# Attention output of head pairs, turned to feature-major by the DMA crossbar instead of TensorE

## The chip, the cores and the metric

The kernel runs on one core of one Trainium2 chip. A core has TensorE (matrix multiplication; the profile splits it into PE, the matmuls, and PEld, the weight loads beside them), VectorE (DVE), ScalarE (ACT), GpSimd (POOL), SyncE (SP, which here only issues DMAs) and 16 DMA engines. Each engine works through its own instruction stream in order and waits for others by semaphores. The metric is the device time in microseconds (us) of one execution; lower is better.

## What is computed

Block-sparse attention over 4 batches of 8 heads (768 tokens, head size 64), followed by a gated feed-forward network with a short convolution along the tokens:

```python
# q, k, v: [4, 8, 768, 64]; mask from neighbouring, first, last and sampled 32-token blocks
scores = where(mask, (q @ k^T) / 8, -1e9)
attn   = softmax(scores)
o      = attn @ v                                   # [4, 8, 768, 64]
x      = o.transpose(0, 2, 1, 3).reshape(4, 768, 512)

h    = maximum(x @ w_in, 0)                         # w_in [512, 1024]
conv = sum over k=0..2 of conv_w[k] * h shifted by k-1 tokens
out  = (h * sigmoid(conv)) @ w_out                  # w_out [1024, 512]
```

Inputs and outputs are float32; the matmuls work on bfloat16.

## The kernel before

The kernel is written in a tile framework: the program lists the operations, and when it is built the framework lays out the order of each engine's stream from dependencies, buffers and its own estimates of durations. So the order in the trace is not always that of the program text.

**Attention, one head per iteration (line 292, 32 iterations).** The loads of q, k and v (lines 57, 58, 64; on GpSimd's DMA queue, with a cast to bfloat16) run three heads ahead. `qk_stage(it+1)` prepares the next head: six TensorE transposes of q and k side by side into the PSUM tile `tq` (line 154) and two VectorE copies to `Qst` and `Kst` (lines 155, 156). `core(i)` works on six key chunks of 128: two matmuls give `st`, the scores of a chunk against all 768 queries (lines 166, 168; the mask is carried in 24 extra rows), ScalarE takes the exponential to `pt` (line 171), and six small matmuls (line 184) add this chunk's part to `o`, a tile [128 tokens, 6, 65] in which column 64 is the sum of the weights. `st` has two buffers, so that the matmuls run one chunk ahead of the exponentials.

**From the attention output to x transposed.** In iteration `it` the output of head `it-1` is finished in three steps. `xstage_a` (line 190): VectorE takes the reciprocal of column 64 (line 193) and multiplies, giving `xtok` [128 tokens, 6, 64] in bfloat16 (line 196). `xstage_b` (line 199): six TensorE transposes by an identity matrix (line 203) into the PSUM tile `tx` [64, 768]. `xstage_c` (line 206): VectorE copies `tx` to the upper or lower 64 rows of `xT[b][fc]` (line 211). Each `xT[b][fc]` is [128 features, 768 tokens] and holds two heads, `fc = h // 2`. `tx` shares its PSUM tag `pmix` (two buffers) with `tq` and with `o2` of the feed-forward network. In the text `xstage_a` stands ahead of `core` and the other two behind it.

**The feed-forward network of batch b runs beside the attention of batch b+1** as fillers handed to `core`. In the first four iterations of its turn (called m1 in this document) `moe1_a` (line 213) multiplies `w_in` with `xT[b][0..3]` to `hp` (lines 217, 219; for each of 8 output chunks, over the 4 feature chunks in order) and ScalarE applies relu to `hT` (line 222); VectorE does the convolution (lines 228 to 231), ScalarE a tanh (line 238), VectorE the gate to `gT` (line 244). The first `moe1_a` of a batch stands one iteration ahead, so it is the first reader of the last `xT` of its batch. In the other four iterations (m2) `moe2` (line 251) multiplies `gT` with `w_out` to `o2` (line 254), VectorE copies it to `o2s` (line 260, two buffers), and SP stores it (line 261). The plan of lines 263 to 287 says which filler goes where; two `moe2` of batch 2 are left for behind the loop (line 323).

**The end.** For batch 3 nothing is left to overlap with. Behind the last head's three steps and the two `moe2` come eight units: matmuls to `lo` and `hi` (lines 338, 340; first readers of `xT[3][3]` at their fourth feature chunk), relu (346, 347), convolution (354, 356, 362, 364), tanh, gate, and the matmuls with `w_out` (369); then six copies (394, 396) and stores (397).

SP's DMA queue carries three small loads at the start, the block indices and the stores.

Of the kernel before, what the change touches and what calls it, by code (L numbers as in the profile page):

```python
# [9 lines left out]
BF16 = mybir.dt.bfloat16  # L10
I32 = mybir.dt.int32
AF = mybir.ActivationFunctionType
ALU = mybir.AluOpType
# [3 lines left out]
def kernel(  # L17
# [11 lines left out]
    nc = tc.nc  # L29

    B, H, S, D = q.shape
    NB = 24
    NCH = S // 128
# [7 lines left out]
    sb = ctx.enter_context(tc.tile_pool(name="sb", bufs=1))  # L41
    ps = ctx.enter_context(tc.tile_pool(name="ps", bufs=1, space=bass.MemoryType.PSUM))
# [7 lines left out]
    xtok_t = {}  # L50
# [19 lines left out]
    ident = sb.tile([128, 128], BF16, tag="ident")  # L70
# [75 lines left out]
    xT = [[sb.tile([128, S], BF16, tag=f"xt{b}_{fc}", name=f"xt{b}_{fc}") for fc in range(NFC)] for b in range(B)]  # L146
# [43 lines left out]
    def xstage_a(i):  # L190
        o = o_t.pop(i)
        rcp = sb.tile([128, NCH], FP32, tag="rcp", bufs=2, name="rcp")
        nc.vector.reciprocal(out=rcp, in_=o[:, :, 64])
        xtok = sb.tile([128, NCH, 64], BF16, tag="xtok", bufs=2, name="xtok")
        rcp_b = rcp.unsqueeze(2).broadcast_to([128, NCH, 64])
        nc.vector.tensor_tensor(out=xtok, in0=o[:, :, 0:64], in1=rcp_b, op=ALU.mult)  # L196
        xtok_t[i] = xtok

    def xstage_b(i):
        xtok = xtok_t[i]  # L200
        tx = ps.tile([64, S], BF16, tag="pmix", bufs=2, name="tx")
        for j in range(NCH):
            nc.tensor.transpose(out=tx[:, 128 * j:128 * j + 128], in_=xtok[:, j, :], identity=ident)  # L203
        xtok_t[i] = tx

    def xstage_c(i):
        b, h = divmod(i, H)
        tx = xtok_t.pop(i)
        fc = h // 2
        r0 = 64 * (h % 2)  # L210
        nc.vector.tensor_copy(out=xT[b][fc][r0:r0 + 64, :], in_=tx[0:64, :])  # L211

    def moe1_a(b, ffc):
        hp = ps.tile([128, S], FP32, tag="st", bufs=2)
# [77 lines left out]
    for it in range(NITER):  # L292
        i = it
        if it + 3 < NHEADS:
            loads(it + 3)
        if it == 3:
            loads_w()
        if it + 1 < NHEADS:
            qk_stage(it + 1)
        if i >= 1:  # L300
            xstage_a(i - 1)

        pe_fill = []
        dve_fill = []
        for bb, ff in m1_of[it + 1]:
            pe_fill.append(lambda bb=bb, ff=ff: moe1_a(bb, ff))
        for bb, tt in m2_of[it]:
            pe_fill.append(lambda bb=bb, tt=tt: moe2(bb, tt))
        for bb, ff in m1_of[it]:
            dve_fill.append(lambda bb=bb, ff=ff: moe1_conv(bb, ff))  # L310

        core(i, pe_fill, dve_fill)
        if i >= 1:
            xstage_b(i - 1)
        for bb, ff in m1_of[it]:
            moe1_gate(bb, ff)
        if i >= 1:
            xstage_c(i - 1)

    xstage_a(NHEADS - 1)  # L320
    xstage_b(NHEADS - 1)
    xstage_c(NHEADS - 1)
    for bb, tt in m2_post:
        moe2(bb, tt, tail=True)
# [103 lines left out]
```

## Time and profile before

| what | value |
|---|---|
| median of 13 runs | 285.08 us |
| lowest and highest run | 282.59 and 286.41 us |
| the profiled execution, whole | 283.37 us |
| its span in the profile | 281.5 us |
| busy: PE, PEld | 241.0 us (86%), 134.6 us (48%) |
| busy: DVE, ACT, POOL | 194.4 us (69%), 202.6 us (72%), 84.5 us (30%) |
| granted TensorE clock, mean | 0.991 |
| DMA packets | 83470, 18.21 MB |

The profile is of one execution. Busy shares are averages over the whole span; matmuls overlap each other in the pipeline, so that a busy PE is not one at its peak. "Releaser" or `<-` names what ended an engine's idle time before an instruction. The chain of waits goes back from the last instruction to what released it at each step. A landing time of a DMA is from its issue to its completion.

By stage the span falls into a start (to about 28 us), attention alone (28 to 65 us), then for each of the batches 0, 1 and 2 an m1 part (from 65, 126 and 187.5 us) and an m2 part (from 98, 160 and 221 us), and the end (from 241.5 us).

### The profile page before, as it was taken

The page shows a single profiled execution, that of the slowest core. Times are in us where ns is not written, and L with a number is a line of the kernel's source. Part 1 is how long each engine was busy: PE and PEld are TensorE (multiplying, and loading weights), DVE is VectorE, ACT ScalarE, POOL GpSimd, SP SyncE. Part 2 cuts the span into 40 slices and gives each one's busy share as a digit, 9 for nine tenths or more (in the row PEclk, how much of TensorE's full clock was granted, in tenths as well). Part 3 has the DMA queues.
Part 4 walks back from the last instruction along what each step waited for, and adds up shares of the span by engine and source line. Part 5 has one row for each costly group of instructions (what it writes and reads, how often), then busy time and mean ns, then how long its engine had stood idle before and what let it go on. Part 6 is the DMA issues. An engine that isn't in the chain of part 4 may idle for free.

```text
span 281.5 us, 5869 instructions
## 1 busy us (share of the span) xinstructions
PE 241.0 (86%) x2370; PEld 134.6 (48%) x2370; DVE 194.4 (69%) x322; ACT 202.6 (72%) x274; POOL 84.5 (30%) x120
## 2 busy tenths in 40 slices
PE   0399898899888999999888999998998999879870
PEld 0145454456544555555555555555565455444320
DVE  0963435437999994457999975449999963259972
ACT  1058888887898986587788976578788966387621
POOL 8993533633423332241333333332111000000000
PEclk9999999999999999999999999999999999999978
DMA  9999997896664494876766585683622011110005
GB/s 52 67 119 163 185 110 48 56 72 45 42 42 30 30 59 91 115 82 41 82 43 44 33 75 82 107 89 55 44 14 16 0 40 75 42 73 1 0 0 224
DMA packets 83470, 18.21 MB, mean 65 GB/s; under 512 B 78836, under 2 KB 79860, under 8 KB 83444
## 3 DMA queue, kind: packets, MB, share of 16 engines
q0 software_dynamic: 76832, 11.54, 57.7%
q1 hardware_dynamic: 6612, 6.31, 6.8%
q8 instruction: 18, 0.29, 0.4%
q14 instruction: 8, 0.07, 0.1%
HBM read 23.08 MB, written 6.29 MB: 104 GB/s over the span
## 4 chain that ended last, share of the span: by engine, by line
PE 60%; ACT 20%; DVE 10%; issue 6%; DMA 2%; SPq 0%; DVEq 0%; ACTq 0%
ACT pt L171 17%; PE o L184 13%; PE st L166 11%; PE o L254 10%; PE hp L217 8%; PE st L168 5%; PE tx L203 4%; PE hp L219 4%; PE tq L154 3%; DVE cv L362 2%; DVE gt L244 2%; DVE cv L364 2%; DMA cw<-in_moe_conv_w_dram 2%; ACT hT L222 1%; ACT tnh L238 1%
## 5 line engine op out<-in xcount | busy, mean ns | idle before, releaser
L171 ACT ACTIVATE pt<-st 128x768 bf16<-128x768 f32 x192 | 149.2, 808 | 42.6 <-PE st L168 37.1
L184 PE MATMUL o<-vp,pt 128*128 128x65 bf16 x1152 | 68.9, 196 | 12.3 <-ACT pt L171 10.7
L166 PE MATMUL st<-qst,kst 88*128 88x512 bf16 x192 | 75.0, 391 | 3.3 <-DVE qst L125 2.3
L184 PEld LDWEIGHTS <-pt 128*128 128x128 bf16 x1152 | 52.0, 98 | 53.9 <-ACT pt L171 41.0
L57 POOL DMA_DIRECT2D qkb<-in_q_dram x32 | 26.7, 833 | 102.8 <-PE tq L154 93.4
L168 PE MATMUL st<-qst,kst 88*128 88x256 bf16 x192 | 53.1, 277 | 0.0
L211 DVE COPY xt<-tx 64x768 bf16<-64x768 bf16 x32 | 17.5, 548 | 35.5 <-PE tx L203 35.4
L254 PE MATMUL o<-woutb,gt 128*128 128x512 bf16 x144 | 35.2, 379 | 0.0
L64 POOL DMA_DIRECT2D vp<-in_v_dram x32 | 26.7, 834 | 26.8 <-PE o L184 25.3
L217 PE MATMUL hp<-xt,winb 128*128 128x512 bf16 x96 | 32.4, 378 | 2.6 <-ACT pt L171 2.5
L244 DVE SCALAR_TENSOR_TENSOR gt<-tnh,hT 128x768 bf16<-128x768 bf16 x32 | 30.3, 949 | 2.1 <-ACT tnh L238 2.1
L238 ACT ACTIVATE tnh<-cv 128x768 bf16<-128x768 bf16 x32 | 26.9, 841 | 5.4 <-DVE cv L364 4.3
L222 ACT ACTIVATE hT<-hp 128x768 bf16<-128x768 f32 x24 | 19.4, 809 | 13.3 <-PE hp L219 12.6
L154 PE MATMUL tq<-ident,qkb 128*128 128x128 bf16 x192 | 21.4, 229 | 7.4 <-POOL ident masks.py:199 7.4
L58 POOL DMA_DIRECT2D qkb<-in_k_dram x32 | 27.0, 843 | 0.0
L219 PE MATMUL hp<-xt,winb 128*128 128x256 bf16 x96 | 26.1, 272 | 0.0
L229 DVE SCALAR_TENSOR_TENSOR cv<-hT,cw,cv 128x767 bf16<-128x767 bf16 x24 | 24.2, 1009 | 0.5
L231 DVE SCALAR_TENSOR_TENSOR cv<-hT,cw,cv 128x767 bf16<-128x767 bf16 x24 | 24.2, 1007 | 0.2
L203 PE MATMUL tx<-ident,xtok 128*64 128x128 bf16 x192 | 22.7, 227 | 0.9 <-DVE xtok L196 0.9
L168 PEld LDWEIGHTS <-kst 88*128 88x128 bf16 x192 | 19.2, 100 | 4.0 <-issue 3.7
L254 PEld LDWEIGHTS <-gt 128*128 128x128 bf16 x144 | 13.9, 97 | 15.0 <-DVE gt L244 0.4
L203 PEld LDWEIGHTS <-xtok 128*64 128x64 bf16 x192 | 13.0, 109 | 16.3 <-issue 11.5
(60 smaller groups left out, 225.0 us busy)
## 6 DMA issues: line engine op xcount, KB each, us to landing
out_dram<-o2s SPq DMA_DIRECT2D x24, 256.0 KB, 2.0
qkb<-in_q_dram POOLq DMA_DIRECT2D x32, 96.0 KB, 3.0
qkb<-in_k_dram POOLq DMA_DIRECT2D x32, 96.0 KB, 3.4
vp<-in_v_dram POOLq DMA_DIRECT2D x32, 96.0 KB, 3.4
winb<-in_moe_w_in_dram POOLq DMA_DIRECT2D x1, 1024.0 KB, 10.5
woutb<-in_moe_w_out_dram POOLq DMA_DIRECT2D x1, 1024.0 KB, 12.4
cw<-in_moe_conv_w_dram SPq DMA_DIRECT2D x3, 4.0 KB, 3.6
sbi<-in_sampled_blocks_dram SPq DMA_DIRECT2D x1, 0.6 KB
```

Source lines behind the costliest of these rows:

```text
L58: nc.gpsimd.dma_start(out=qkb[:, :, 64:128], in_=k[b, h].rearrange("(c p) d -> p c d", p=128))
L154: nc.tensor.transpose(out=tq[:, 128 * c:128 * c + 128], in_=qkb[:, c, :], identity=ident)
L166: nc.tensor.matmul(out=st[:, 0:512], lhsT=kchunk, rhs=Qst[par][0:88, 0:512], start=True, stop=True)
L168: nc.tensor.matmul(out=st[:, 512:768], lhsT=kchunk, rhs=Qst[par][0:88, 512:768], start=True, stop=True)
L171: nc.scalar.activation(out=p, in_=st, func=AF.Exp, bias=0.0, scale=0.125)
L184: nc.tensor.matmul(out=o[:, j, 0:65], lhsT=ptc[:, 128 * j:128 * j + 128], rhs=Vp[par][:, c, 0:65], start=(c == 0 and j == 0), stop=(c == N ...
L203: nc.tensor.transpose(out=tx[:, 128 * j:128 * j + 128], in_=xtok[:, j, :], identity=ident)
L217: nc.tensor.matmul(out=hp[:, 0:512], lhsT=lw, rhs=xT[b][fc][:, 0:512], start=(fc == 0), stop=(fc == NFC - 1), skip_group_check=True)
L219: nc.tensor.matmul(out=hp[:, 512:768], lhsT=lw, rhs=xT[b][fc][:, 512:768], start=(fc == 0), stop=(fc == NFC - 1), skip_group_check=True)
L238: nc.scalar.activation(out=tnh, in_=cv, func=AF.Tanh, bias=0.0, scale=0.5)
L244: nc.vector.scalar_tensor_tensor(out=gT[ffc], in0=tnh, scalar=1.0, in1=hT, op0=ALU.add, op1=ALU.mult)
L254: nc.tensor.matmul(out=o2, lhsT=gT[ffc][:, 128 * t:128 * t + 128], rhs=woutb[:, ffc, :], start=(ffc == 0), stop=(ffc == NFFC - 1), skip_gr ...
```

## The change

Two heads share one `xtok` tile of [128 tokens, 6, 128]: the even head writes columns 0 to 63 of each chunk, the odd head columns 64 to 127. After the odd head one DMA on SP's queue, with the crossbar's transpose, reads the pair's tile as [128, 768] and writes `xT[b][h // 2]` whole, as [128 features, 6, 128 tokens]. The six TensorE transposes of each head, the PSUM tile `tx` and the VectorE copy are gone; the even head's `xstage_b` and both heads' `xstage_c` do nothing. `xtok` keeps two buffers, which are now pairs of heads.

```diff
         rcp = sb.tile([128, NCH], FP32, tag="rcp", bufs=2, name="rcp")
         nc.vector.reciprocal(out=rcp, in_=o[:, :, 64])
-        xtok = sb.tile([128, NCH, 64], BF16, tag="xtok", bufs=2, name="xtok")
+        if i % 2 == 0:
+            xtok_t[i // 2] = sb.tile([128, NCH, 128], BF16, tag="xtok", bufs=2, name="xtok")
+        xtok = xtok_t[i // 2]
+        r0 = 64 * (i % 2)
         rcp_b = rcp.unsqueeze(2).broadcast_to([128, NCH, 64])
-        nc.vector.tensor_tensor(out=xtok, in0=o[:, :, 0:64], in1=rcp_b, op=ALU.mult)
-        xtok_t[i] = xtok
+        nc.vector.tensor_tensor(out=xtok[:, :, r0:r0 + 64], in0=o[:, :, 0:64], in1=rcp_b, op=ALU.mult)
 
     def xstage_b(i):
-        xtok = xtok_t[i]
-        tx = ps.tile([64, S], BF16, tag="pmix", bufs=2, name="tx")
-        for j in range(NCH):
-            nc.tensor.transpose(out=tx[:, 128 * j:128 * j + 128], in_=xtok[:, j, :], identity=ident)
-        xtok_t[i] = tx
+        if i % 2 == 0:
+            return
+        b, h = divmod(i, H)
+        xtok = xtok_t.pop(i // 2)
+        nc.sync.dma_start_transpose(
+            out=xT[b][h // 2][:, :].rearrange("p (c s) -> p c s", c=NCH),
+            in_=xtok[:, :, :].rearrange("p c s -> p (c s)"))
 
     def xstage_c(i):
-        b, h = divmod(i, H)
-        tx = xtok_t.pop(i)
-        fc = h // 2
-        r0 = 64 * (h % 2)
-        nc.vector.tensor_copy(out=xT[b][fc][r0:r0 + 64, :], in_=tx[0:64, :])
+        pass
```

## The prediction, made before the changed kernel was timed

> **What bounds the kernel now.** First the page: its chain of waits by line.
>
> ```profile
> span 281.5 us, 5869 instructions
> ...
> ACT pt L171 17%; PE o L184 13%; PE st L166 11%; PE o L254 10%; PE hp L217 8%; PE st L168 5%; PE tx L203 4%; PE hp L219 4%; PE tq L154 3%; DVE cv L362 2%; DVE gt L244 2%; DVE cv L364 2%; DMA cw<-in_moe_conv_w_dram 2%; ACT hT L222 1%; ACT tnh L238 1%
> ```
>
> No line has a fifth of the chain; TensorE and ScalarE hand over to each other. The line that goes, L203, has 4%. An average over stages says little, so next comes busy time by stage: 28 to 65 us (attention alone), 65 to 98 (attention beside the first FFN half, "m1"), 98 to 126 (attention beside the second, "m2"). Columns: length, busy time (count) of PE, PEld, DVE, ACT, POOL, then clock, DMA share, GB/s.
>
> ```profile
> 28.00:65.00 37.00, 33.63 (x422) 18.19 (x421) 17.03 (x36) 32.90 (x43) 17.42 (x22) 1.00 1.12 90
> 65.00:98.00 33.00, 29.83 (x305) 17.86 (x305) 30.03 (x48) 28.43 (x39) 10.77 (x15) 1.00 0.58 38
> 98.00:126.00 28.00, 26.98 (x282) 15.04 (x283) 17.08 (x32) 19.87 (x27) 9.10 (x12) 1.00 0.77 89
> ```
>
> In the first ScalarE sets the pace, in m1 three engines are near full, in m2 TensorE is. The chain by line for each stage, in that order, then m1 and m2 of the next two batches (126, 160, 187.5, 221 to 241.5 us):
>
> ```profile
> by line: PE o L184 26.0%; PE st L166 20.0%; ACT pt L171 19.9%; PE tx L203 13.0%; PE st L168 10.4%; PE tq L154 8.4%; issue 2.5%; ACTq L171 0.4%
> ...
> by line: ACT pt L171 26.1%; PE hp L217 23.9%; PE hp L219 10.7%; PE o L184 10.3%; issue 7.4%; PE st L166 7.4%; PE tx L203 5.2%; PE tq L154 3.8%; PE st L168 3.8%; ACT hT L222 3.1%; ACTq L171 0.2%; ACT tnh L238 0.2%
> ...
> by line: PE o L254 32.4%; ACT pt L171 20.5%; PE o L184 16.4%; PE st L166 13.2%; PE st L168 6.9%; PE tq L154 4.7%; issue 3.5%; PE tx L203 2.9%; ACTq L171 0.3%
> ...
> by line: ACT pt L171 25.6%; PE hp L217 23.3%; PE o L184 10.5%; PE hp L219 10.4%; issue 9.2%; PE st L166 7.8%; PE st L168 4.0%; ACT hT L222 3.0%; PE tx L203 3.0%; PE tq L154 2.3%; ACT tnh L238 1.5%; PE o L254 1.3%; ACTq L171 0.1%
> ...
> by line: PE o L254 32.2%; ACT pt L171 23.8%; PE o L184 15.6%; PE st L166 12.7%; PE st L168 7.0%; PE tq L154 3.2%; issue 3.2%; PE tx L203 2.9%; ACTq L171 0.3%
> ...
> by line: PE hp L217 23.7%; ACT pt L171 23.5%; PE hp L219 10.6%; PE o L184 10.3%; issue 9.2%; PE st L166 7.3%; PE st L168 3.7%; ACT hT L222 3.1%; PE tx L203 3.1%; PE tq L154 2.3%; PE o L254 1.9%; ACT tnh L238 1.5%; ACTq L171 0.1%
> ...
> by line: PE o L254 34.3%; PE o L184 17.4%; ACT pt L171 16.0%; PE st L166 13.8%; PE st L168 7.2%; PE tx L203 3.9%; PE hlo L338 2.9%; issue 2.3%; PE tq L154 2.2%; ACTq L171 0.3%
> ```
>
> L203 is on the path in every stage, never for much.
>
> **The change part by part.** Removed are the 192 transposes and 32 copies of these groups (busy time and mean ns, then the engine's idle time before them and what ended it):
>
> ```profile
> L211 DVE COPY xt<-tx 64x768 bf16<-64x768 bf16 x32 | 17.5, 548 | 35.5 <-PE tx L203 35.4
> ...
> L203 PEld LDWEIGHTS <-xtok 128*64 128x64 bf16 x192 | 13.0, 109 | 16.3 <-issue 11.5 <-DVE o2s L260 2.5 <-DVE xtok L196 1.3
> ```
>
> The 17.5 us of VectorE I count at nothing before the tail: L211 waited 35.4 us for TensorE, so it ran in idle VectorE time, and it is on no stage's chain. On m1's full VectorE it is a margin and no term: conv and gate would come earlier, and nothing on that chain waits for them. TensorE time counts only where nothing else is late. With the transposes go their waits for a PSUM buffer that they share with o2 (2.5 us behind o2s); tq takes such a buffer too and may inherit them, so I count none of it and keep 2.5 for the low end.
>
> *Attention alone, 28 to 65 us.* One head's boundary:
>
> ```profile
> 42.05 0.24 PE L203 MATMUL tx<-ident,xtok 128*64 128x128 bf16 x1
> 42.23 0.34 PE L154 MATMUL tq<-ident,qkb 128*128 128x128 bf16 x3
> ...
> 42.75 0.38 PE L166 MATMUL st<-qst,kst 88*128 88x512 bf16 x1
> ...
> 43.34 0.81 ACT L171 ACTIVATE pt<-st 128x768 bf16<-128x768 f32 x1 [0.31 <-PE st L168]
> ```
>
> ScalarE idles 0.31 us per head because st starts late, and one transpose stands before it: 42.23-42.05 = 0.18 us. The other five lie under exponentials. The chain's 13.0% of 37 us (4.8) can't be had, as only 7 x 0.31 = 2.2 us of idle ScalarE exist. Seven heads x 0.18: **1.2 us** (0 to 2.2).
>
> *m1 and m2.* Chain share times length: 0.052x33 = 1.7, 0.029x28 = 0.8, 0.030x34 = 1.0, 0.029x27.5 = 0.8, 0.031x33.5 = 1.0, 0.039x20.5 = 0.8; sum 6.2. An m1 example shows that this is real:
>
> ```profile
> 75.57 0.52 PE L203 MATMUL tx<-ident,xtok 128*64 128x128 bf16 x6
> ...
> 76.42 0.38 PE L217 MATMUL hp<-xt,winb 128*128 128x512 bf16 x1
> ...
> 77.92 0.81 ACT L222 ACTIVATE hT<-hp 128x768 bf16<-128x768 f32 x1 [0.85 <-PE hp L219]
> ```
>
> Six transposes hold hp back while ScalarE idles 0.85 us for it. But each hole closed brings up the next path: the row shows hp released 0.85 us late, of which the transposes are at most 0.52, so other waits remain behind. And the order on TensorE is laid out when the program is built: a head's six transposes stand scattered in attention alone (x1 at 42.05) and in a row in m1 (x6 at 75.57). Without them the planner may put tq, hp or st elsewhere, for better or worse. Between none and all of 6.2 I take three quarters, as most pieces stand before such an idle ScalarE: **4.6 us**.
>
> *Added: 16 crossbar DMAs on SP.* No row shows one. Its pieces are 256 bytes (128 bf16), 768 of them; a load of v or q is 768 rows of 64 float32, also 256 bytes each. Landing times, min/median/max, of the v loads, the q loads and the stores:
>
> ```profile
> DMA to landing us min/median/max: 3.0/3.4/9.3
> ...
> DMA to landing us min/median/max: 2.8/3.0/9.4
> ...
> DMA to landing us min/median/max: 2.0/2.0/3.6
> ...
> q0 software_dynamic: 76832, 11.54, 57.7%
> ```
>
> So a landing L lies between 2.0 and 9.4 us; I take 3.4, the row with as many pieces of the same size. [...] Traffic grows by 16 x 768 = 12,288 packets, at q0's rate 9% of the span; the loads it meets are issued three heads ahead, over 15 us by 37 us for seven heads, which is more than the slowest 9.4. If that cover went, st would wait for a late tq.
>
> SP's queue holds only stores. Where does xT have to be there? At the fourth feature chunk of the first hp of each batch:
>
> ```profile
> 60.10 0.56 DVE L196 TENSOR_TENSOR xtok<-o,rcp 128x384 bf16<-128x384 f32 x1
> ...
> 66.16 0.38 PE L217 MATMUL hp<-xt,winb 128*128 128x512 bf16 x1
> ...
> 121.16 0.69 DVE L260 COPY o2s<-o 128x512 f32<-128x512 f32 x1 [0.75 <-PE o L254]
> ...
> 127.02 0.38 PE L217 MATMUL hp<-xt,winb 128*128 128x512 bf16 x1
> ...
> 182.83 0.69 DVE L260 COPY o2s<-o 128x512 f32<-128x512 f32 x1 [1.03 <-PE o L254]
> ...
> 188.68 0.38 PE L217 MATMUL hp<-xt,winb 128*128 128x512 bf16 x1
> ...
> L261 SPq DMA_DIRECT2D out_dram<-o2s x18: 332/332/367, 105.9 to 247.2; - x18
> ```
>
> Batch 0: 66.16-60.66 = 5.5 us of cover. In batches 1 and 2 the DMA stands in program order behind that iteration's store, which waits for its copy and takes 0.33 us to issue: 127.02-122.18 and 188.68-183.85, 4.8 us each. Behind a DMA on SP wait only later stores. Its issue I price as a store's, 0.33 us, with SP held until the landing (9.4) as the other end: then stores would start that much later, and with two o2s buffers the second copy after it, and so TensorE's o2, would wait. 0.33 is the nearest row, of the same queue. The new wait of xtok for the DMA two pairs earlier has four heads, 21 us, of cover. xtok's write is half-row strided with the same 384 elements from PSUM; I take no change (L196 takes 0.56 us per head, so a 10% change would be 1.8 us of VectorE, mostly idle).
>
> *The end.*
>
> ```profile
> 241.20 0.36 PE L184 MATMUL o<-vp,pt 128*128 128x65 bf16 x6
> 241.82 0.56 DVE L196 TENSOR_TENSOR xtok<-o,rcp 128x384 bf16<-128x384 f32 x1
> 242.43 0.52 PE L203 MATMUL tx<-ident,xtok 128*64 128x128 bf16 x6 [0.88 <-DVE xtok L196]
> 242.89 3.63 PE L254 MATMUL o<-woutb,gt 128*128 128x512 bf16 x16
> ...
> 246.84 0.33 PE L338 MATMUL hlo<-xt,winb 128*128 128x384 bf16 x1
> ```
>
> L254 need no longer wait for tx: it can start at 241.56, and hlo 246.84-242.89 = 3.95 us behind it, at 245.5, if xT is there. The DMA lands at 242.38+L = 245.8. hlo then runs 246.84-245.8 = **1.0 us** earlier; break-even is L = 4.5, and beyond it the end is later by L-4.5, for everything behind follows from hlo.
>
> **Sum:** 1.2+4.6+1.0 = 6.8 us. The profiled execution took 283.37 (span 281.5, 1.9 around it) and would take 276.6; it lies 1.7 below the median 285.08, which becomes 278.3.
>
> **Rivals.**
> *Cover:* the transposes fill holes in which TensorE waits for exponentials anyway.
>
> ```profile
> 116.09 2.46 ACT L171 ACTIVATE pt<-st 128x768 bf16<-128x768 f32 x3 [1.43 <-PE st L168]
> ...
> 116.43 0.47 PE L203 MATMUL tx<-ident,xtok 128*64 128x128 bf16 x5
> 116.96 0.36 PE L184 MATMUL o<-vp,pt 128*128 128x65 bf16 x6
> ```
>
> Here the o matmuls wait for the exponential that ends at 116.91 whatever tx does. Against it stands the 0.85 us hole above. If only the end gains: 285.1-1.0 = 284.1.
>
> *Late landing, the slower side:* L eats the covers 5.5, 4.8, 4.8 and 4.5 (together 19.6). TensorE, in order, stalls 4L-19.6 while the transposes removed still give 5.8: it decides from L = 6.35 on. With the slowest load's L = 9.4 the stalls are 18.0, the time 285.1+12.2 = 297.3. For it: 9.4 occurs, and a transpose may be slower than a copy. Against: that is a load queued behind weights, and at the end no load runs. [...]
>
> *Not what it says:* the DMA breaks into single elements, 128 times the pieces. At q0's rate (57.7% of 281.5 us for 76,832) 1.57 million pieces take 3.3 ms. Nothing but the change's words speaks against it.
>
> **How the numbers follow.** Forecast 0.55, 278.3, own range 274 to 283; cover 0.17, 284.1; late landing 0.26; not what it says 0.02. A measurement of this kernel can tell 0.5%, 1.4 us, from no change. Cover splits half and half between faster and same; late landing leaves 0.04 near its break-even. Faster 0.55+0.08 = 0.63, same 0.09+0.04 = 0.13, slower 0.22+0.02 = 0.24. Low end 273: all of 2.2 and 6.2, 1.3 at the end with L = 2.0 (hlo right at 245.5), and the 2.5 of buffer waits, 12.5 in all, give 272.6, rounded up. High end 289: L = 7.3; beyond it lies some 0.1.
>
> **What would show it.** ScalarE's idle per head below 0.31 us in attention; idle before hT below 0.85 in m1; L by the DMA rows; no stall of hp L217 on a DMA at the three batch starts; hlo right behind L254 at the end. I am wrong if L exceeds 6, or if TensorE's busy time falls with ScalarE's idle time unchanged.

## The result: right in total, by two errors that cancel

The changed kernel takes 278.73 us (median of 11 runs, 276.25 to 280.82) against 285.42 us for the kernel before (48 runs): a ratio of 0.9783, 95% interval 0.9749 to 0.9817, clear of no change and on both sides of a gain of 2%. (Medians are of all runs; the ratios leave out slow ones, those more than 1.5% above the fastest of their kernel.) Predicted were 278.3 us and a range of 273 to 289. The steps to that number were worse than the number: the m2 parts gained six times what they were given (11.7 us for 1.8), m1 gained nothing, and a stall that had no term stands at the start.

From the page of the changed kernel; its profiled execution took 278.73 us as well:

```profile
span 277.0 us, 5494 instructions
...
PE 226.2 (82%) x2178; PEld 123.9 (45%) x2178; DVE 177.3 (64%) x290; ACT 202.0 (73%) x274; POOL 84.7 (31%) x120
...
PEclk9999957999999999999999799999999999999997
...
DMA packets 96270, 21.35 MB, mean 77 GB/s; under 512 B 91636, under 2 KB 92660, under 8 KB 96244
...
q1 hardware_dynamic: 19412, 9.45, 14.2%
...
ACT pt L171 19%; PE o L184 12%; PE st L166 9%; PE o L254 9%; PE hp L217 8%; PE st L168 5%; PE hp L219 4%; DMA qkb<-in_k_dram 4%; ACT hT L222 3%; DVE cv L362 2%; DVE gt L244 2%; DVE cv L364 2%; DMA cw<-in_moe_conv_w_dram 2%; ACT tnh L238 2%; PE tq L154 1%
```

L203 has left the chain of waits, but a load has come into it: `qkb<-in_k_dram`, the k of some head, with 4%. And the clock row has two dents, slices 6 and 7 and slice 23.

To see where the time went, the span is cut at the starts of the VectorE reciprocal (line 193) of the same heads in every kernel: those of heads 3, 8, 12, 16, 20, 24, 28 and 31. The columns are the start, attention alone (five heads), m1 and m2 of batches 0, 1 and 2 (the last m2 has three heads), the end, and the span, in us. Each row is one profiled execution; the experiments, told below, stand in it too.

| kernel | start | att. | m1 b0 | m2 b0 | m1 b1 | m2 b1 | m1 b2 | m2 b2 | end | span |
|---|---|---|---|---|---|---|---|---|---|---|
| before | 38.89 | 26.20 | 33.00 | 27.81 | 33.74 | 27.92 | 33.75 | 20.28 | 39.91 | 281.5 |
| after | 47.19 | 25.00 | 33.27 | 22.90 | 34.63 | 23.99 | 33.36 | 17.41 | 39.25 | 277.0 |
| e1_w_later | 42.61 | 25.01 | 33.27 | 22.91 | 33.36 | 24.01 | 33.36 | 17.41 | 38.96 | 270.9 |
| e2_q2 | 38.70 | 26.19 | 36.59 | 24.93 | 34.35 | 24.20 | 33.99 | 17.97 | 38.98 | 275.9 |
| e3_dma_twice | 49.55 | 25.02 | 33.27 | 22.91 | 33.36 | 24.01 | 33.35 | 17.42 | 38.81 | 277.7 |
| e4_pairs_on_pe | 36.30 | 25.43 | 35.42 | 24.75 | 33.13 | 25.45 | 33.13 | 18.27 | 41.42 | 273.3 |
| e5_w_gate | 37.27 | 25.00 | 33.27 | 22.91 | 33.35 | 24.01 | 33.35 | 17.41 | 38.93 | 265.5 |
| e6_buffer | 39.52 | 25.05 | 34.32 | 26.45 | 35.90 | 26.93 | 37.56 | 21.02 | 40.25 | 287.0 |
| e7_tq_twice | 35.86 | 24.99 | 33.78 | 24.57 | 35.26 | 23.82 | 35.04 | 15.95 | 39.13 | 268.4 |
| e8_copy | 37.24 | 25.00 | 33.74 | 22.43 | 33.27 | 25.21 | 33.26 | 18.61 | 38.94 | 267.7 |
| e9_before_gate | 40.96 | 26.21 | 33.04 | 27.80 | 33.74 | 27.92 | 33.74 | 20.29 | 39.90 | 283.6 |
| e10_pairs_gate | 39.80 | 25.42 | 35.45 | 24.75 | 33.13 | 25.45 | 33.13 | 18.27 | 39.80 | 275.2 |
| e11_dummy_first | 38.68 | 25.02 | 33.72 | 22.91 | 33.35 | 24.01 | 33.37 | 17.41 | 39.63 | 268.1 |

After minus before: start +8.3, attention alone -1.2, m1 +0.3, +0.9 and -0.4, m2 -4.9, -3.9 and -2.9, end -0.7; together -4.5, the difference of the spans. The medians differ by 6.7: the profiled execution of before, 283.37 us, was 2 us faster than its median, that of after stood at its own.

**The start.** TensorE's timeline of after, around its longest idle time:

```profile
31.24 0.27 PE L168 MATMUL st<-qst,kst 88*128 88x256 bf16 x1
38.98 0.37 PE L154 MATMUL tq<-ident,qkb 128*128 128x128 bf16 x2 [7.47 <-DMA qkb<-in_k_dram]
...
39.49 0.62 PE L166 MATMUL st<-qst,kst 88*128 88x512 bf16 x1
```

TensorE stands still for 7.47 us before the tq of a later head, and the st of the current head, whose data are there, waits behind it in the stream. Then st takes 0.62 us in place of 0.38. The windows of the same time (length, busy time and count of PE, PEld, DVE, ACT, POOL, clock, DMA share, GB/s) show the clock of 0.51 that follows:

```profile
31.00:39.00 8.00, 0.53 (x9) 0.17 (x6) 1.11 (x2) 1.40 (x2) 3.75 (x5) 0.73 1.80 166
39.00:45.00 6.00, 6.00 (x52) 4.23 (x52) 0.76 (x2) 3.24 (x4) 2.46 (x3) 0.51 1.71 111
```

Why is k late? GpSimd's timeline has its loads in order:

```profile
19.93 0.85 POOL L140 DMA_DIRECT2D winb<-in_moe_w_in_dram  x1
...
24.09 0.89 POOL L141 DMA_DIRECT2D woutb<-in_moe_w_out_dram  x1
...
24.97 0.83 POOL L57 DMA_DIRECT2D qkb<-in_q_dram  x1
28.19 0.82 POOL L64 DMA_DIRECT2D vp<-in_v_dram  x1 [2.39 <-PE o L184]
29.00 0.83 POOL L58 DMA_DIRECT2D qkb<-in_k_dram  x1
```

The two weights, 1 MB each, are issued at 19.93 and 24.09. The k load issued at 29.00 (counted along the queue, head 7's) is behind them and is waited for until 38.98. In the kernel before nobody needed it then. The windows with tile tq alone, up to the end of the start stage, count the tq transposes, six to a head, in before and in after:

```profile
0.00:38.89 38.89, 4.61 (x36) 1.00 1.40 118
```

```profile
0.00:47.19 47.19, 8.31 (x54) 0.89 1.44 116
```

By head 3's output, before has made tq for 36 / 6 = 6 heads, after for 54 / 6 = 9. The load of k kept its time (before issues it at 29.07); its reader moved three heads ahead.

**m2.** The windows of m2 of batch 0, before and after:

```profile
98.09:125.90 27.81, 26.79 (x282) 14.92 (x282) 16.92 (x31) 19.71 (x27) 8.91 (x12) 1.00 0.77 89
```

```profile
105.46:128.36 22.90, 21.83 (x242) 12.31 (x241) 10.63 (x21) 19.02 (x26) 8.21 (x10) 1.00 0.86 111
```

TensorE is busy for 96% of it before and 95% after: m2 lasts as long as TensorE has work in it. What work that is, the groups by line of the same windows say (busy time and mean ns, then idle time before); before:

```profile
L254 PE MATMUL o<-woutb,gt 128*128 128x512 bf16 x42 | 10.1, 379 | 0.0
...
L154 PE MATMUL tq<-ident,qkb 128*128 128x128 bf16 x24 | 2.7, 221 | 0.0
L203 PE MATMUL tx<-ident,xtok 128*64 128x128 bf16 x24 | 2.7, 226 | 0.0
```

and after:

```profile
L254 PE MATMUL o<-woutb,gt 128*128 128x512 bf16 x31 | 9.6, 379 | 0.0
...
L154 PE MATMUL tq<-ident,qkb 128*128 128x128 bf16 x18 | 2.2, 219 | 0.0
```

Not only the 24 transposes went. Eleven o2 matmuls and six tq transposes left the stage too; the same view of after's m1 of batch 0 has the o2 matmuls, of which before has none there:

```profile
L254 PE MATMUL o<-woutb,gt 128*128 128x512 bf16 x12 | 3.9, 378 | 0.0
```

What one of them costs TensorE is read from rows in which they stand close together, six tx in 0.52 us (at 75.57, in the prediction), six tq in 0.51, eight o2 in 1.89:

```profile
76.02 0.51 PE L154 MATMUL tq<-ident,qkb 128*128 128x128 bf16 x6
...
113.59 1.89 PE L254 MATMUL o<-woutb,gt 128*128 128x512 bf16 x8
```

That is 0.087, 0.085 and 0.24 us. Batch 0: 24 x 0.087 + 6 x 0.085 + 11 x 0.24 = 2.1 + 0.5 + 2.6 = 5.2 us, against 4.9 measured. The counts of all stages, taken in the same way (o2 / tq / tx):

| kernel | m1 b0 | m2 b0 | m1 b1 | m2 b1 | m1 b2 | m2 b2 |
|---|---|---|---|---|---|---|
| before | 0/24/24 | 42/24/24 | 8/24/24 | 42/24/24 | 8/24/24 | 32/6/18 |
| after | 12/12/0 | 31/18/0 | 11/30/0 | 38/18/0 | 11/30/0 | 33/0/0 |
| e2_q2 | 2/24/0 | 42/18/0 | 6/30/0 | 42/18/0 | 6/30/0 | 38/0/0 |
| e4_pairs_on_pe | 4/28/12 | 38/18/12 | 11/30/12 | 38/18/12 | 11/30/12 | 28/0/6 |
| e5_w_gate | 11/12/0 | 27/18/0 | 10/30/0 | 34/18/0 | 9/30/0 | 30/0/0 |
| e9_before_gate | 0/24/24 | 38/24/24 | 7/24/24 | 38/24/24 | 7/24/24 | 30/6/18 |
| e6_buffer | 0/24/4 | 38/24/4 | 6/24/4 | 38/24/4 | 6/24/4 | 30/6/3 |
| e7_tq_twice | 11/26/0 | 27/36/0 | 18/60/0 | 25/36/0 | 18/60/0 | 22/0/0 |

Records are missing in the last four rows: the whole run has 144 o2 matmuls, all of them recorded in the first four kernels, but 129 in e5_w_gate and e7_tq_twice and 133 in e9_before_gate and e6_buffer. So those four are compared only with each other; e9_before_gate has the stage times of before to 0.04 us from attention on, but 38 o2 where before has 42. For batches 1 and 2 the same sum gives 3.6 and 1.8 us, against 3.9 and 2.9. Of the 11.7 us, 66 transposes are 5.7 and work that moved out of m2 is 4.9 (18 tq, 14 o2); 1.1 us are left over.

**m1.** The hole that the prediction took for its example, with what stands before it; before:

```profile
75.57 0.52 PE L203 MATMUL tx<-ident,xtok 128*64 128x128 bf16 x6
75.58 0.79 ACT L222 ACTIVATE hT<-hp 128x768 bf16<-128x768 f32 x1
```

and the same place in after:

```profile
82.28 0.81 ACT L222 ACTIVATE hT<-hp 128x768 bf16<-128x768 f32 x1
...
83.15 0.38 PE L217 MATMUL hp<-xt,winb 128*128 128x512 bf16 x1
...
84.64 0.81 ACT L222 ACTIVATE hT<-hp 128x768 bf16<-128x768 f32 x1 [0.85 <-PE hp L219]
```

The hole is 0.85 us in both. hp starts 0.06 us after the preceding hT ends (82.28 + 0.81 = 83.09), and in before 0.05 us after it (75.58 + 0.79 = 76.37, hp at 76.42): hp and st share one PSUM tag with two buffers (lines 164 and 214), and hp waits for ScalarE to free one. The six tx were over at 76.09, and the six tq of the row at 76.02 follow them; but without either, the buffer was not free before 76.37.

**The landing.** The source's own rows for the DMA (issue time in ns, then the landing):

```profile
L206 SPq DMA_TRANSPOSE xt<-xtok x16: 1212/1223/1667, 28.7 to 238.6; - x16
...
  PE hlo L338: 0.7, 1
...
DMA to landing us min/median/max: 2.7/3.5/8.6
```

Only the first hlo waited for it, 0.7 us, once; no hp did.

### The profile page after: what moved, and what is told of

The parts are those of the page before. It is cut to its first block, busy times and chain, and to the rows that moved or that the text cites. A ratio compares the mean times of both kernels' runs of the same rounds, so it can differ in the third digit from the quotient of the medians.

```text
span 277.0 us, 5494 instructions
## 1 busy us (share of the span) xinstructions
PE 226.2 (82%) x2178; PEld 123.9 (45%) x2178; DVE 177.3 (64%) x290; ACT 202.0 (73%) x274; POOL 84.7 (31%) x120
## 2 busy tenths in 40 slices
DMA packets 96270, 21.35 MB, mean 77 GB/s; under 512 B 91636, under 2 KB 92660, under 8 KB 96244
## 4 chain that ended last, share of the span: by engine, by line
PE 48%; ACT 25%; DVE 10%; issue 8%; DMA 6%; SPq 1%; POOL 0%; DVEq 0%; ACTq 0%
ACT pt L171 19%; PE o L184 12%; PE st L166 9%; PE o L254 9%; PE hp L217 8%; PE st L168 5%; PE hp L219 4%; DMA qkb<-in_k_dram 4%; ACT hT L222 3%; DVE cv L362 2%; DVE gt L244 2%; DVE cv L364 2%; DMA cw<-in_moe_conv_w_dram 2%; ACT tnh L238 2%; PE tq L154 1%
## 5 line engine op out<-in xcount | busy, mean ns | idle before, releaser
L254 PE MATMUL o<-woutb,gt 128*128 128x512 bf16 x144 | 41.7, 379 | 0.0
L155 DVE COPY qst<-tq 64x768 bf16<-64x768 bf16 x32 | 17.5, 547 | 33.1 <-PE st L168 24.1
L217 PE MATMUL hp<-xt,winb 128*128 128x512 bf16 x96 | 33.6, 388 | 3.7 <-ACT hT L222 1.6
L154 PE MATMUL tq<-ident,qkb 128*128 128x128 bf16 x192 | 23.9, 237 | 15.2 <-DMA qkb<-in_k_dram 7.7
L154 PEld LDWEIGHTS <-qkb 128*128 128x128 bf16 x192 | 16.4, 106 | 24.4 <-issue 18.1
L219 PE MATMUL hp<-xt,winb 128*128 128x256 bf16 x96 | 26.7, 278 | 0.0
L193 DVE RECIPROCAL rcp<-o 128x6 f32<-128x6 f32 x32 | 6.2, 193 | 26.6 <-PE o L184 26.2
L168 PEld LDWEIGHTS <-kst 88*128 88x128 bf16 x192 | 19.3, 100 | 5.5 <-issue 5.4
L166 PEld LDWEIGHTS <-kst 88*128 88x128 bf16 x192 | 19.1, 100 | 2.5 <-issue 0.6
```

Of the source, the lines that this page charges most:

```text
L154: nc.tensor.transpose(out=tq[:, 128 * c:128 * c + 128], in_=qkb[:, c, :], identity=ident)
L166: nc.tensor.matmul(out=st[:, 0:512], lhsT=kchunk, rhs=Qst[par][0:88, 0:512], start=True, stop=True)
L168: nc.tensor.matmul(out=st[:, 512:768], lhsT=kchunk, rhs=Qst[par][0:88, 512:768], start=True, stop=True)
L217: nc.tensor.matmul(out=hp[:, 0:512], lhsT=lw, rhs=xT[b][fc][:, 0:512], start=(fc == 0), stop=(fc == NFC - 1), skip_group_check=True)
L219: nc.tensor.matmul(out=hp[:, 512:768], lhsT=lw, rhs=xT[b][fc][:, 512:768], start=(fc == 0), stop=(fc == NFC - 1), skip_group_check=True)
L254: nc.tensor.matmul(out=o2, lhsT=gT[ffc][:, 128 * t:128 * t + 128], rhs=woutb[:, ffc, :], start=(ffc == 0), stop=(ffc == NFFC - 1), skip_gr ...
```

## The experiments

The theory after the first readings: **(P)** the gain is the order of TensorE's stream, in which work can move to better places because nothing of the attention output takes one of the two `pmix` buffers any more; **(W)** its price is that tq runs ahead into loads that queue behind the weights. The rivals: TensorE's time itself (T), VectorE's time (V), the landing (L).

**Weights later.** The request for both weights moved from iteration 3 to 6.

```diff
-        if it == 3:
+        if it == 6:
             loads_w()
```

> The changed kernel with the two weight loads listed three heads later. Theory A (the 7.5 us stall of TensorE at 31.5 us is a k load that queues behind the 2 MB of weights, met because tq now runs several heads ahead): the stall shrinks to 0 to 3 us, the clock stays up, and the time is 270.5 to 273.5. Rival B (the stall comes from the crossbar DMA that starts at 28.7 us beside the loads): the stall stays, 277.5 to 280.

Measured: 274.07 us (4 runs), ratio 0.9639 [0.9569, 0.9709]; start 42.61 in place of 47.19. A stall is left:

```profile
32.03 0.48 PE L154 MATMUL tq<-ident,qkb 128*128 128x128 bf16 x3 [3.53 <-DMA qkb<-in_k_dram]
```

In this execution `woutb` was issued at 30.20, but `winb`, which waits for nothing, still at 19.83. So half of the stall goes with one of the two weights. The time lies between the two brackets: W is supported, not yet settled.

**Shorter lead.** Qst and Kst get two buffers in place of four, so that tq cannot run three heads ahead; the loads stay as in the changed kernel.

```diff
+    NQK = 2
-    Qst = [... for p in range(NPAR)]
-    Kst = [... for p in range(NPAR)]
+    Qst = [... for p in range(NQK)]
+    Kst = [... for p in range(NQK)]
...
-        par = i % NPAR
+        par = i % NQK
```

> The changed kernel with two buffers in place of four for the prepared q and k of a head, so that tq can't run more than about two heads ahead; the weight loads stay where they are. Theory A: the stall goes, 270 to 273. Rival B: it stays, 277.5 to 280, as the crossbar DMAs are the same.

Measured: 277.96 us, 0.9794 [0.9719, 0.987]: a miss in total. The start fell to 38.70 as W expects, but the order changed elsewhere: attention alone is back at 26.19, m2 b0 at 24.93, and m1 b0 took 36.59, with st at 0.62 us from 73.4 to 76.5 and again from 82.9 to 86.4. The edit changes more than the lead, and it shows something of m2. No tx transposes stand there and `pmix` is as free as in the changed kernel, but the o2 matmuls have not moved; the group in m2 of batch 0:

```profile
L256 PE MATMUL o<-woutb,gt 128*128 128x512 bf16 x42 | 11.7, 378 | 0.0
```

That is 42 as in before, and m1 of batch 0 has 24 tq again and only 2 o2 (counts above). By the prices above 24 tx and 6 tq are 2.6 of the 2.9 us between 27.81 and 24.93. So the free buffer alone does not move o2; the longer lead of tq, which this edit cuts, seems to be needed too.

**Twice the transposes by DMA.** Behind each real one a second goes into a tile that nothing reads.

```diff
+        xdum = sb.tile([128, S], BF16, tag="xdum", bufs=2, name="xdum")
+        nc.sync.dma_start_transpose(
+            out=xdum[:, :].rearrange("p (c s) -> p c s", c=NCH),
+            in_=xtok[:, :, :].rearrange("p c s -> p (c s)"))
```

> The changed kernel with each crossbar DMA issued twice, the second into a tile that nobody reads; the order on the engines is that of the changed kernel. If the DMAs run beside everything: within 1 us of the changed kernel, 277.7 to 279.7, with 0.3 to 1.2 us more at the end if the second holds up the first's landing. Rival B: the stall at 31.5 us grows by 1 us or more and SP's 1.2 us per issue delays stores, 281 or more.

Measured: 279.29 us, 0.9827 [0.9771, 0.9883], hardly more than the changed kernel. The table shows it stage by stage: the start is 2.4 us longer, no other stage by more than 0.1. TensorE's wait there:

```profile
PE tq L154 <- DMA qkb<-in_k_dram: 9.8, 1, 9.8
```

9.8 us in place of 7.5. The doubled crossbar traffic goes with a late k load that is later by another 2.3 us, as rival B said of the stall, and costs nothing where loads have cover, so that the total stays in the first bracket. How much of the 7.5 us is the first crossbar DMA's, and not the weights', no run separates.

**Packing without the crossbar.** Two heads share `xtok`, but six TensorE transposes [128 by 128] and one VectorE copy [128, 768] turn the pair.

```diff
-        nc.sync.dma_start_transpose(
-            out=xT[b][h // 2][:, :].rearrange("p (c s) -> p c s", c=NCH),
-            in_=xtok[:, :, :].rearrange("p c s -> p (c s)"))
+        tx = ps.tile([128, S], BF16, tag="pmix", bufs=2, name="tx")
+        for j in range(NCH):
+            nc.tensor.transpose(out=tx[:, 128 * j:128 * j + 128], in_=xtok[:, j, :], identity=ident)
...
+        nc.vector.tensor_copy(out=xT[b][h // 2], in_=tx)
```

> Packing alone: the pair's tile is turned by six 128x128 TensorE transposes and one 128x768 VectorE copy, so half of the removed work of both engines stays, and no crossbar DMA. If the gain goes with TensorE and VectorE work, half of it: 281 to 283, if not more from a stall that is absent. If it goes with the PSUM buffers that the transposes share with tq and o2, less than half: 283 to 285.

Measured: 273.81 us, 0.9632 [0.9566, 0.9698]: both expectations missed, and the version is 4.9 us faster than the one with the crossbar. `pmix` is taken by tx 16 times in place of 32; m2 falls to 24.75, 25.45 and 18.27, about two thirds of the way (76.0 before, 68.5 here, 64.3 after, summed over the batches): half of the transposes are still there, but as many tq as in the changed kernel, and 4 o2 per batch, have left m2 (counts above). And tq does not run far enough ahead to meet a late load (start 36.30).

**Weights held back.** The changed kernel with `winb` requested after head 4's xtok and `woutb` after head 8's; a one-element copy into each makes the load wait (`loads_w` is split in two).

```diff
-        if it == 3:
-            loads_w()
+        if it == 5:
+            nc.vector.tensor_copy(out=winb[0:1, 0, 0:1], in_=xtok_t[(i - 1) // 2][0:1, 0, 0:1])
+            loads_w1()
+        if it == 9:
+            nc.vector.tensor_copy(out=woutb[0:1, 0, 0:1], in_=xtok_t[(i - 1) // 2][0:1, 0, 0:1])
+            loads_w2()
```

> The changed kernel with the two weight loads held back: w_in until head 4 has been written to xtok, w_out until head 8 (a one-element VectorE copy into each ahead of its load). Theory A (loads behind the 2 MB of weights make the stall in the start, 8.3 us by the end of head 3): the start is as before (38 to 39.5 us to the reciprocal of head 3) or earlier and the time is 267.5 to 271. Rival B (the crossbar DMA beside the loads makes it): above 274, the start above 42.

Measured: 268.42 us (267.39 to 269.38), 0.9434 [0.9346, 0.9522], the fastest kernel of this study, 10.3 us under the changed one. The stall is gone, and the windows with tile tq alone show that the lead stayed:

```profile
0.00:37.27 37.27, 7.35 (x54) 1.00 1.44 91
```

So W holds: 54 transposes by head 3 as in after, but no late load, and the start is 9.9 us shorter (47.19 - 37.27): 7.5 of idle TensorE, and 2.4 for which the 6 us at a clock of 0.51 are the likely reason. The second dent of the clock row went too (m1 b1 33.35 in place of 34.63).

**The same for the kernel before, as a control.** The same edit, in the kernel before.

> The kernel before with the weights held back as in e5_w_gate, nothing else. Theory G (the gate only takes away the stall and the crowd of loads that the change brought; the kernel before has neither): start within 1.5 us of its 38.9, the other stages as before, 282.5 to 285.5 us. Rival H (the gate is worth the same 10 us to any version, and then the gain of e5_w_gate says nothing of the change): 273 to 277 us.

Measured: 285.17 us, 1.0011 [0.9964, 1.0058]. G holds: the gate gives the kernel before nothing. Its start is 2.1 us longer in the profiled execution, more than expected; the likely reason is that st is at 0.38 us only from 30.55 on, in before from 24.41 (told at the end). The cost that the gate removes came with the change.

**One buffer per head put back.** e5_w_gate with one small transpose per head into a `pmix` tile and a copy of 64 by 16 out of it, which nothing reads.

```diff
+        tx = ps.tile([64, S], BF16, tag="pmix", bufs=2, name="tx")
+        for j in range(1):
+            nc.tensor.transpose(out=tx[:, 128 * j:128 * j + 128], in_=xt2[:, j, 64 * (i % 2):64 * (i % 2) + 64], identity=ident)
...
+        nc.vector.tensor_copy(out=scr[0:64, 0:16], in_=tx[0:64, 0:16])
```

> e5_w_gate, and each head again takes one of the two shared PSUM buffers for a moment: one of the six transposes (0.08 us of TensorE) and a VectorE copy of 64x16; the result is not used. Theory P (the gain beside the second FFN half, some 4 us per batch, comes from the PSUM buffers that tq and o2 no longer share with the transposes, and so from another order on TensorE): 6 to 11 us slower than e5_w_gate, m2 back near 27 us. Rival T (it comes from TensorE's time): at most 1.5 us slower.

Measured: 287.28 us (10 runs), 1.0081 [1.0029, 1.0133]: by the ratios some 18 us above e5_w_gate, with a sixth of the transposes and a copy of 16 columns per head put back. In the profiled execution the granted clock is 0.95 in m1 of batch 1 and 0.91 and 0.92 in batch 2, so only the parts at 1.00 are used: m2 26.45 and 26.93 for batches 0 and 1, against 22.91 and 24.01 without and 27.81 and 27.92 in the kernel before. The tq count up to head 3's output is that of before:

```profile
0.00:39.52 39.52, 5.35 (x36) 1.00 1.08 69
```

The o2 matmuls in m2 of batch 0, in e5_w_gate and then here:

```profile
L256 PE MATMUL o<-woutb,gt 128*128 128x512 bf16 x27 | 8.6, 379 | 0.1
```

```profile
L264 PE MATMUL o<-woutb,gt 128*128 128x512 bf16 x38 | 9.7, 378 | 0.1
```

38 is what e9_before_gate has there, and in the other stages o2 and tq are those of e9_before_gate too, to one o2. So it is the taking of a buffer, not the size of the work done in it, that decides where o2 and tq stand, and P holds for the placing. By the prices above, 11 o2, 6 tq and 4 tx are 11 x 0.24 + 6 x 0.085 + 4 x 0.087 = 3.5 us, all of the difference in m2 of batch 0 (26.45 - 22.91); in batch 1 4 o2, 6 tq and 4 tx are 1.8 of the 2.9 us, and what the rest is stays open. The 18 us as a whole are more than P expected; m1 at 35.90 and 37.56 ran at a clock of 0.95 and 0.91, so not all of it is order.

**TensorE's time put back, without the buffer.** e5_w_gate with the transposes of q and k each done twice into the same tile: 192 more, as many as the change removed.

```diff
-        for c in range(NCH):
+        for c in list(range(NCH)) * 2:
```

> e5_w_gate, with each transpose of q and k done twice into the same place: TensorE's removed work (six transposes per head) is there again, but no further buffer is taken. Rival T: 5 to 9 us slower than e5_w_gate, m2 back near 27 us. Theory P: 1 to 4 us slower.

Measured: 270.59 us, 0.9506 [0.944, 0.9572]: 2.2 us more. T alone is out: with all of TensorE's work back but no buffer taken, by the ratios some 14 of the 16 us between before and e5_w_gate remain. The counts show how: in m1 of batch 1 there are 60 tq transposes (35.26 us in place of 33.35), and 9 more o2 matmuls have left m2 of batch 1 (25 for 34 in e5_w_gate), which in spite of 18 more tq takes 23.82 us for 24.01. That m2 follows TensorE's work holds here too: in batch 0, where o2 stays, 18 more tq are 1.5 us, and 24.57 - 22.91 = 1.7.

**VectorE's time put back.** e5_w_gate with a copy of 64 by 768 per head, from Kst, which nothing reads.

```diff
+        nc.vector.tensor_copy(out=scr[0:64, :], in_=Kst[i % NPAR][0:64, :])
```

> e5_w_gate, with a VectorE copy of 64x768 per head (from SBUF, about 0.5 us, result unused) where the removed one stood. Theories P and T: within 1 us of e5_w_gate. Rival V (the gain is VectorE's 17.5 us): 3 us slower or more, most of it in m1, where VectorE is at 91%.

Measured: 272.76 us (269.84 to 273.26, 4 runs), 0.9557 [0.947, 0.9645]: 4.3 us more by the medians. The copies from SBUF are shorter than those removed, which took 17.5 us:

```profile
L214 DVE COPY scr<-kst 64x768 bf16<-64x768 bf16 x32 | 12.1, 378 | 0.3
```

The profiled execution is the fastest of the four, and there m1 is as without the copy but for 0.5 us in batch 0, while m2 changes by -0.5, +1.2 and +1.2. V's place, m1, is not supported; that the copies cost nothing isn't either. In m2 of batch 1 VectorE is busy for only 14.9 of the 25.2 us, TensorE has the same 34 o2 and 18 tq as in e5_w_gate, and it waits 2.2 us for exponentials in place of 1.0: the price there is a wait, not a full VectorE. What made that wait, and why the other three runs are 3 us longer, stays open.

**Packing without the crossbar, weights held back.** e4_pairs_on_pe with the gate of e5_w_gate, so that the two can be compared without a stall.

> The packing alone (TensorE transposes and a copy per pair, as e4_pairs_on_pe) with the weights held back as in e5_w_gate, so that neither it nor e5_w_gate has the stall at the start. Theory P (most of the gain comes from freeing the PSUM buffers half as often, the crossbar itself gives the end, 1.5 to 2.5 us, and 1 to 2 us per m2): 271.5 to 274 us, m2 24 to 25.5 us per batch. Rival X (the crossbar gives nothing over packing beside the end): 269.5 to 271 us. Rival T (TensorE time is what counts; half of it is back): 275 to 278 us.

Measured: 275.16 us, 0.9658 [0.9583, 0.9733]. By the total this is T's bracket, by the stages P's: m2 24.75, 25.45 and 18.27, exactly as in e4_pairs_on_pe. Against e5_w_gate it loses 0.4 in attention alone, 2.2 in m1 b0 (granted clock 0.95 in that window), 4.1 in the three m2, 0.9 at the end, and 2.5 at the start, where st is slow until 32.1; the two other m1 are 0.2 us shorter each. Its profiled execution is the slowest of the four, 2.2 us above the median, so these add up to more than the medians differ by. So the crossbar on its own is worth about 6.7 us by the medians (275.16 - 268.42), or 5.4 against the same packing without the gate (273.81); 5.4 of the profiled differences are in attention, m2 and the end. It is worth that only where the loads don't stall it. T's reading, that half of TensorE's time is back, is not separated from the placing by this run alone.

**A later landing.** e5_w_gate with a dummy crossbar DMA ahead of each real one.

```diff
+        nc.sync.dma_start_transpose(
+            out=xdum[:, :].rearrange("p (c s) -> p c s", c=NCH),
+            in_=xtok[:, :, :].rearrange("p c s -> p (c s)"))
         nc.sync.dma_start_transpose(
```

> e5_w_gate with a second crossbar DMA of the same pair, into a tile that nothing reads, issued ahead of each real one, so that xT lands later by at least one issue (1.2 us) and at most one landing (4 us). Theory C (the covers at the batch starts, 4.8 to 5.5 us behind a landing of 4.0, still hold or nearly; only the end follows the landing): the end later by 1 to 4 us, at most 1 us at each batch start, 269.5 to 273 us. Rival L (the landing is already on the path at each batch start): three stalls of 1 to 4 us on the DMA of xt there besides, 274 to 284 us.

Measured: 271.76 us, 0.9539 [0.9479, 0.9599]. TensorE's waits for the landing, in the view of waits (us in total, times, longest):

```profile
PE hlo L348 <- DMA xt<-xtok: 1.6, 1, 1.6
...
PE hp L223 <- DMA xt<-xtok: 0.3, 1, 0.3
```

C holds in the main: with the real DMA issued 1.3 us later, two batch starts still see nothing and one sees 0.3 us; the last hlo waits 1.6 us in place of 0.4. The end grows by 0.7, less than the 1 to 4 that C expected, and the start by 1.4. The medians differ by 3.3 us, at the upper part of C's bracket.

## Why the prediction was right, and where it wasn't

*Attention alone, 1.2 us:* the stage is 1.2 us shorter. From 52.81 on ScalarE has 17 exponentials in a row without waiting for TensorE:

```profile
52.81 13.99 ACT L171 ACTIVATE pt<-st 128x768 bf16<-128x768 f32 x17 [0.20 <-ACT pt L171]
```

The mechanism was right: the 0.31 us in which ScalarE waited at each head are gone. That the figures agree is in part luck: the prediction has seven heads at 0.18 us, the stage as cut here has five, at 0.24.

*m1, three quarters of 3.7 = 2.8 us:* measured +0.8, or about -0.5 where no clock dent comes in (100.49 before, 99.97 in e5_w_gate). The failed step is the reading of the example: "Six transposes hold hp back while ScalarE idles 0.85 us for it." The six stood ahead of hp in the stream, but hp started 0.05 us behind the end of hT, whose buffer it takes. The chain of waits charged the transposes 5.2% because it steps from an instruction to the one before it on its engine. The room on TensorE that 24 transposes and 12 tq left in batch 0 was filled with 12 o2 matmuls of m2. That the buffer makes the hole is read from rows; a third buffer for st wasn't tried.

*m2, three quarters of 2.4 = 1.8 us:* measured 11.7. Two steps failed. The size was the transposes' share of the chain of waits (0.8 us in batch 0). The chain steps through some of the instructions of a full engine, and the share counts only those; the same text says that in m2 TensorE is the limit, and there all 24 count, 2.1 us. That makes 5.7 for the three stages. The other step is "tq takes such a buffer too and may inherit them, so I count none of it", with "the planner may put tq, hp or st elsewhere, for better or worse" and no price: the freed buffer let o2 and tq leave m2 for stages where TensorE had room, 4.9 us by the counts. e6_buffer shows that it takes the buffer (the placing goes back, with 3.5 us in m2 of batch 0), e2_q2 that it is not the buffer alone (the lead of tq seems to be needed as well), e7_tq_twice that it is more than TensorE's time (2.2 us when all of it is put back elsewhere).

*The loads, at nothing:* "the loads it meets are issued three heads ahead, over 15 us". True when it was read, and undone by the same freedom: tq moved by three heads, and the cover was gone. The warning that followed, that "st would wait for a late tq", named what happened but had no term; it cost 9.9 us at the start (after against e5_w_gate).

*The end, 1.0 us:* 0.7. hlo runs right behind L254, as foretold, and waits at its fourth feature chunk:

```profile
238.56 1.22 SPq L206 DMA_TRANSPOSE xt<-xtok  x1
239.92 0.33 PE L338 MATMUL hlo<-xt,winb 128*128 128x384 bf16 x1
...
241.76 0.32 PE L338 MATMUL hlo<-xt,winb 128*128 128x384 bf16 x1 [0.70 <-DMA xt<-xtok]
```

*The crossbar:* L was taken as 3.4 us, the author's estimate from the v loads, as no row of before shows such a DMA; the median is 3.5. 12,288 packets more were expected, 12,800 found (96270 - 83470), so the DMA is what it says. Its issue was priced as a store's 0.33 us and takes 1.22; SP has the time, so the term stayed at nothing. The stores of 256 KB on the same queue land in 2.2.

*VectorE's 17.5 us at nothing:* left open. e8_copy, with 12.1 us of copies put back, is 4.3 us slower by the medians, though not in m1 and not where VectorE is full.

*The rivals.* Late landing fell: no batch start waited, and e11_dummy_first shows room for 1.3 us more, nearly. Cover was right in its core for m1, where a buffer's wait covered the transposes, and wrong in m2.

*The signs.* Neither of the two signs of being wrong came: the median L is 3.5 us (the longest 8.6), and ScalarE's idle time fell with TensorE's busy time, from 78.9 (281.5 - 202.6) to 75.0 us. But the sign named for m1, idle before hT below 0.85 us, didn't come either: it is 0.85 in both.

*The range.* The four terms of the low end, 2.2, 6.2, 1.3 and 2.5, add up to 12.2 and not 12.5; that gives 272.9 and rounds to the same 273.

The two large errors, 9.9 us too little gain in m2 and 8.3 us at the start without a term, are of opposite sign and share a cause, the work that moved when `pmix` came free; m1, 3.6 us short of its 2.8, takes up most of the rest. That the total came out is luck: without the stall the change is worth some 16 us (ratio 0.9434, 268.42 us), below the low end of the range.

## What to carry to other kernels

In a stage where one engine is full, price every instruction that leaves it in full, not by its share of the chain of waits; and where an operation leaves a shared PSUM tag in a kernel whose order is planned at build time, ask which other users of the tag can now move, out of which stage, and what they meet there. Check the cover of every load against where its reader may move to, not where it stands now. Before a hole is charged to the instructions that stand ahead of it, compare its end with the release of the buffer that the waiting instruction takes.

## What the runs showed of the hardware

*The clock after an idle stretch.* Behind the 7.5 us of idle TensorE the windows above give a clock of 0.51 for 6 us, with TensorE busy throughout. In e1_w_later, behind 3.53 us of idle TensorE, the slow stretch was shorter: TensorE works again from 32.03 on, and st is down to 0.47 us at 34.91 and to 0.38 at 35.82. A dent also came without a long gap (0.74 us, before the hp at 154.12), in after's m1 of batch 1:

```profile
152.00:154.00 2.00, 1.15 (x15) 0.47 (x12) 1.73 (x3) 2.00 (x4) 1.47 (x2) 1.00 0.96 61
154.00:156.00 2.00, 1.88 (x7) 0.84 (x7) 1.98 (x4) 1.50 (x3) 0.17 (x1) 0.52 1.40 95
```

TensorE was busy 1.15 of 2.0 us just before. e1_w_later, e3_dma_twice and e5_w_gate run this stage in 33.36, 33.36 and 33.35 us without it, so it costs 1.3 us and isn't in the order alone.

*The slow phase at the start varies.* Every profiled execution begins with st at 0.58 to 0.63 us, and the change to 0.38 came between 16.5 us (e7_tq_twice) and 32.1 us (e10_pairs_gate). In e9_before_gate st stayed slow until 30.55:

```profile
25.63 0.62 PE L168 MATMUL st<-qst,kst 88*128 88x512 bf16 x1
...
30.55 0.38 PE L168 MATMUL st<-qst,kst 88*128 88x512 bf16 x1
```

The clock column of the windows shows 1.00 there (in before from 15 to 25 us, with TensorE busy for 9.74 of the 10 us and st at 0.59 to 0.62 up to 22.4), so the durations have to be read. This moves the start of single executions by 2 to 3.5 us (e9_before_gate against before, e10_pairs_gate against e4_pairs_on_pe) and is a reason to compare stages, not spans.

*The crossbar DMA.* A [128, 768] tile in bfloat16 takes 1.22 us to issue on SP's queue, 800 packets (12,800 / 16), and 2.7 to 8.6 us to land, 3.5 in the median.
